# Thresholded attention with a SoLU feed-forward: q and k loaded in strips and turned on VectorE from the third batch on

## The chip, the cores and the metric

The kernel runs on one core of a Trainium2 chip. The time is the device time of one execution in microseconds (us). The kernel before was run three times: 895.34, 896.09 and 898.36 us, a median of 896.09 us.

## What is computed

For 8 batches of 8 heads, with q, k and v of 576 rows of 64 float32 each, attention keeps only the scores that lie within tau of their row's maximum. Its result is the input of a feed-forward block with a softmax-weighted activation and a layer norm:

```python
scores = scale * np.matmul(q, k.transpose(0, 1, 3, 2))          # scale = 1/8
thresh = np.max(scores, axis=-1, keepdims=True) - tau
scores = np.where(scores >= thresh, scores, -1000000000.0)
attn = np.exp(scores - np.max(scores, axis=-1, keepdims=True))
attn = attn / (np.sum(attn, axis=-1, keepdims=True) + 1e-09)
attn_out = np.matmul(attn, v)                                    # 8 x 8 x 576 x 64
x = attn_out.transpose(0, 2, 1, 3).reshape(4608, 512)
h = x @ w_in                                                     # 512 -> 1024
solu = h * softmax(h)
out = layer_norm(solu) * g_ln @ w_out                            # 1024 -> 512
```

## The kernel before

**Rounds.** The work is cut into 144 rounds (`slots`), 18 for each batch. Rounds 0 to 15 of a batch take one pair of heads and 128 of the first 512 query rows each (`kind` 0 and 1, `hp`, `r`); rounds 16 and 17 take the last 64 query rows of all heads (`kind` 2). In a round, `scores` (L412) makes the scores of both heads in two PSUM tiles `s_ps`, 128 x 576 each. `maxes` (L434, VectorE) finds each row's maximum and adds tau, `ramp` (L449, ScalarE) reads the scores a second time and pushes everything below the threshold far down, `exps` (L458, ScalarE) takes the exponential and its row sum. The score tiles are free for the next round once both ramps have read them. One round later `normalise` (L465 to L468, GpSimd) divides by the sum and `blocks` (L480, VectorE) turns the weights in blocks of 32 x 32 into T. After every second round T goes into its final place wT by four SyncE DMAs (L491). `attend_steps` (L516) multiplies wT by v some rounds later into `pv`, which ScalarE copies to `xh` or `xe` (L539).

**Feed-forward.** A tile of 128 tokens takes four rounds: two halves of h (`ff_h`, L572) and two halves of o (`ff_o`, L676). Between them lie the row maximum (L587), the exponential (L596, ScalarE), the product (L602), the statistics (L617, L618, then GpSimd), the norm (L638 on ScalarE, L643 on VectorE), a swap of halves by four SyncE DMAs (L654), and a 32 x 32 block transpose (L664). ScalarE copies the result out (L691) and SyncE stores it (L703). A pv product runs only in rounds without a half of o.

**q, k and v.** The matmuls need q and k with the 64 values of a row along the partitions. `load_one` (L129) brings four heads of q or k, rows of four tokens (1,024 bytes) to a partition, `load_ends` (L140) the last 64 rows in runs of 256 bytes, both on SyncE from the second batch on. They are turned on TensorE by 64 x 64 matmuls with the identity (`turn`, L282), 36 for each pair of heads (each shows as two records), into columns of the score tiles that the scores leave free. `q_item`, `k_item` and `e_item` then copy them out of PSUM: q times `scl` (the scale, with its sign, or 0) on ScalarE (L315) and VectorE (L319), k on both (L340), the ends on ScalarE (L356) and VectorE (L360). `load_v` brings v in one DMA of 128 rows and two of 64 rows with runs of 1,024 bytes (L159), and two with runs of 256 bytes (L164).

**What sets the order.** Every engine works through its own instructions in the order in which the main loop writes them. A round writes, in this order: `begin` jobs (the copy of the last o), scores with the items that `preps` has due, maxes, ramps, keeps (the copies of turned q and k), exps, `normalise` of the round before, `middle` jobs, the feed-forward quarter, the pv that is due, `blocks` of the round before, `late` jobs, and the loads that `load_at` lists for this round. `preps` lists for each pair of heads the round from which it may be turned, four to twelve rounds ahead of its first use. Buffers: `loads` holds two tiles each for q and k and three for v, `heads` seven each for the turned q and k.

The factor and the threshold are applied here:

```python
nc.vector.tensor_scalar(out=scl, in0=tau_t, scalar1=0.0, scalar2=SCALE, op0=ALU.is_ge, op1=ALU.mult)
...
nc.vector.tensor_tensor_reduce(out=w, in0=ps[:, 0:S], in1=(zero if loose else tau_t).to_broadcast([P, S]), scale=1.0, ...)
...
nc.scalar.activation(out=d["w"][x], in_=..., func=AF.Prelu, bias=d["nth"][x], scale=-1.0, alpha=1.0e30)
```

Of the kernel before, what the change touches and what calls it, by code (L numbers as in the profile page):

```python
# [8 lines left out]
F32 = mybir.dt.float32  # L9
# [11 lines left out]
def kernel(  # L21
# [56 lines left out]
    ntau = const.tile([P, 1], F32, name="ntau")  # L78
    scl = const.tile([P, 1], F32, name="scl")
    g_rows = const.tile([NC, P], F32, name="g_rows")  # L80
# [9 lines left out]

    halves = {}
    ends = {}
    pairs = {}
# [26 lines left out]
    def load_one(b, hf, nm, queue=None):  # L120
# [6 lines left out]
        for x, part in enumerate(parts):  # L127
# [5 lines left out]
            if hf == 0 and x == 0:  # L133
                if b not in ends:
                    ends[b] = loads.tile([P, H, D], F32, tag="ends", name="ends")
                load_ends(b, nm, slice(0, 2) if len(parts) > 1 else slice(0, H), queue)

    def load_ends(b, nm, of, queue):
        src, rows = {"q": (q, ROWS[0]), "k": (k, ROWS[1])}[nm]
        queue.dma_start(  # L140
            out=ends[b][rows, of], in_=src[b, of, SM:S, :].rearrange("h p d -> p h d")
        )
# [5 lines left out]
    def load_v(b, hf, parts=(0, 1, 2)):  # L148
        d = halves.setdefault((b, hf), {})
        hs = slice(4 * hf, 4 * hf + 4)  # L150

        if 0 in parts:
            d["v"] = loads.tile([P, 4, NK, D], F32, tag="v", bufs=3, name="v")
# [14 lines left out]
    def constants():  # L168

        nc.gpsimd.memset(lim, 0.0)  # L170
        nc.scalar.activation(out=ntau, in_=lim, func=AF.Exp)
        make_identity(nc, ident)
        nc.gpsimd.memset(mhalf, -0.5)
        nc.gpsimd.memset(mone, -1.0)
        nc.gpsimd.memset(zero, 0.0)
        nc.gpsimd.memset(lim, -896.0 * 8388608.0)

        nc.vector.tensor_scalar(  # L180
            out=scl, in0=tau_t, scalar1=0.0, scalar2=SCALE, op0=ALU.is_ge, op1=ALU.mult
        )
        nc.vector.tensor_scalar(
            out=tau_t, in0=tau_t, scalar1=0.0, scalar2=104.0, op0=ALU.max, op1=ALU.min
        )
        nc.vector.tensor_scalar(out=ntau, in0=tau_t, scalar1=-1.0, scalar2=None, op0=ALU.mult)

    def gains():
# [106 lines left out]
    def pair(i):  # L295
        if i not in pairs:
            pairs[i] = dict(
                qT=heads.tile([P, SM], F32, tag="qT", name="qT"),
                kT=heads.tile([P, S], F32, tag="kT", name="kT"),
                qe=heads.tile([P, ST], F32, tag="qe", name="qe"),  # L300
            )
        return pairs[i]

    def q_item(i, ts=slice(0, 4)):
# [8 lines left out]
        def keep(spare, x, r):  # L313
            if r == 0 or spare.get("eased"):
                nc.scalar.activation(  # L315
                    out=qT[:, r, ts], in_=seen(spare, r, x, n), func=AF.Copy, scale=scl
                )
            else:
                nc.vector.tensor_scalar(  # L319
                    out=qT[:, 1, ts], in0=seen(spare, 1, x, n), scalar1=scl, scalar2=None,  # L320
                    op0=ALU.mult,
                )

# [23 lines left out]
    def e_item(i):  # L347
# [6 lines left out]
        def keep(spare, x, r):  # L354
            if r == 0:
                nc.scalar.activation(  # L356
                    out=pair(i)["qe"], in_=seen(spare, 0, x, 1)[:, 0], func=AF.Copy, scale=scl
                )
            else:
# [63 lines left out]
    def maxes(s, loose):  # L423
# [4 lines left out]
        for ps in d["ps"]:  # L428
            if loose:
                nth = both[:, len(d["w"]) : len(d["w"]) + 1]  # L430
            else:
                nth = small.tile([P, 1], F32, tag="nth", name="nth")
            w = work.tile([P, S], F32, tag="w", bufs=4, name="w")
            nc.vector.tensor_tensor_reduce(  # L434
                out=w, in0=ps[:, 0:S], in1=(zero if loose else tau_t).to_broadcast([P, S]), scale=1.0, scalar=BIG,
                op0=ALU.add, op1=ALU.min, accum_out=nth,
# [10 lines left out]
    def ramp(s, x):  # L447
        d = live[s]
        nc.scalar.activation(  # L449
            out=d["w"][x], in_=d["w"][x] if d["loose"] else d["ps"][x][:, 0:S], func=AF.Prelu, bias=d["nth"][x], scale=-1.0,  # L450
            alpha=1.0e30,
# [43 lines left out]
    def attend_steps(key):  # L495
# [7 lines left out]
        for e in range(2) if kind == 2 else [None]:  # L503
            for m in range(NK):
                for u in range(2):
                    d, h0 = source(b * NP + (hp if e is None else e + 2 * u))
                    for h in range(2):
# [3 lines left out]
                        else:  # L511
# [4 lines left out]
                        nc.tensor.matmul(  # L516
                            out=to, lhsT=d["v"][ROWS[u], h0 + h, m ^ 4 * u if m < 8 else m],
                            rhs=rhs,
# [175 lines left out]
    def ff_store(t, last):  # L694
# [3 lines left out]
        else:  # L698
            b, kind, m = t
            rows = out[b * S : b * S + SM, :].rearrange("(p t) m -> t p m", t=4)  # L700
            rows = rows[2 * kind + m].rearrange("(r k) m -> k r m", r=2)
# [20 lines left out]
    preps = []  # L722
    for i in range(NP, NPAIR):
        b, hp = divmod(i, NP)
        if b == 1:
            at = (13, 15, 19, 20)[hp]
        else:
            at = PER * (b - 1) + ((6, 12, 16, 21) if b == 2 else (6, 9, 12, 17))[hp]
        preps += [
# [6 lines left out]
    load_at = {}  # L736
    for b in range(1, B):
        r = PER * (b - 1)

        for at, job, hf, what in (  # L740
            (-1 if b > 1 else 11, load_one, 0, "q"),
            (1 if b > 1 else 9, load_one, 0, "k"),
            (7 if b > 1 else 13, load_one, 1, "k"),
            (9 if b > 1 else 15, load_one, 1, "q"),
            (11 if b > 1 else 17, load_v, 0, (0,)),
            (13 if b > 1 else 19, load_v, 0, (1, 2)),
            (PER + 3, load_v, 1, (0,)),
            (PER + 5, load_v, 1, (1, 2)),
        ):
            load_at.setdefault(r + at, []).append(  # L750
                lambda b=b, job=job, hf=hf, what=what: job(b, hf, what)
            )

    with tc.manual_schedule():
# [29 lines left out]
        while True:  # L784
# [120 lines left out]
            if rnd - 1 in live:  # L905
                blocks(rnd - 1)
            for job in late.pop(rnd, []):
                job()
# [49 lines left out]
```

## Time and profile before

| | |
|---|---|
| median of three runs | 896.09 us (895.34 to 898.36) |
| the profiled execution | 897.51 us; its span, first to last instruction, 895.6 us |
| mean granted TensorE clock | 0.972 |
| DMA packets | 95,502, 154.61 MB, mean 173 GB/s |
| of these on SyncE's queue | 94,192, 150.09 MB |
| copies of turned q and k on ScalarE from PSUM (L315, L340, L356), mean | 475, 317 and 225, 339 ns |
| the same on VectorE (L319, L340, L360), mean | 479, 352 and 216, 215 ns |
| DMA of wT (L491), issue to landing | 3.9 / 5.7 / 9.9 us (least, median, most) |

A line of the profile names engine, source line, operation, the tile written and the tiles read. PE is TensorE, PEld its weight loads, DVE VectorE, ACT ScalarE, POOL GpSimd, SP SyncE; a "q" behind an engine is its sequencer, which waits, branches and issues DMAs. "idle before" is time in which the engine stood still ahead of the instruction, with what ended it. In the row of DMA each digit is the busy share of the DMA engines in one fortieth of the span, in tenths. Matmuls overlap each other, so the busy times of groups on PE can't be added to a time on the path.

### The profile page before, as it was taken

The page shows a single profiled execution, that of the slowest core. Times are in us where ns is not written, and L with a number is a line of the kernel's source. Part 1 is how long each engine was busy: PE and PEld are TensorE (multiplying, and loading weights), DVE is VectorE, ACT ScalarE, POOL GpSimd, SP SyncE. Part 2 cuts the span into 40 slices and gives each one's busy share as a digit, 9 for nine tenths or more (in the row PEclk, how much of TensorE's full clock was granted, in tenths as well). Part 3 has the DMA queues.
Part 4 walks back from the last instruction along what each step waited for, and adds up shares of the span by engine and source line. Part 5 has one row for each costly group of instructions (what it writes and reads, how often), then busy time and mean ns, then how long its engine had stood idle before and what let it go on. Part 6 is the DMA issues. An engine that isn't in the chain of part 4 may idle for free. (4 is left out here: it accounts for less than half of the span.)

```text
span 895.6 us, 39683 instructions
## 1 busy us (share of the span) xinstructions
PE 849.5 (95%) x17089; PEld 653.5 (73%) x17089; DVE 679.9 (76%) x1312; ACT 591.0 (66%) x1241; POOL 450.9 (50%) x871
## 2 busy tenths in 40 slices
PE   5668899999999999999999999999999999999997
PEld 3445577877677777777688887887778787777655
DVE  5999886888777778777777877777777877887351
ACT  5766776777767767776677776677766776676121
POOL 2546555555555555555645555555555555555120
PEclk9678899999999999999999999999999999999999
DMA  7999879786877777777777767866887766766322
GB/s 240 248 225 264 208 196 210 181 209 161 207 164 172 162 177 170 185 171 167 189 178 173 172 158 183 184 172 158 189 184 176 183 131 143 167 142 131 79 48 48
DMA packets 95502, 154.61 MB, mean 173 GB/s; under 512 B 27224, under 2 KB 69216, under 8 KB 95328
## 3 DMA queue, kind: packets, MB, share of 16 engines
q1 hardware_dynamic: 94192, 150.09, 71.8%
q8 instruction: 134, 2.20, 1.1%
q10 hardware_dynamic: 1136, 2.00, 0.7%
q14 instruction: 40, 0.33, 0.1%
HBM read 46.14 MB, written 9.44 MB: 62 GB/s over the span
## 5 line engine op out<-in xcount | busy, mean ns | idle before, releaser
L434 DVE CUSTOM_DVE_ANT_0 w<-s_ps,tau_t 128x576 f32<-128x576 f32 x280 | 200.7, 754 | 138.3 <-PE s_ps L412 114.4
L449 ACT ACTIVATE w<-s_ps,nth 128x576 f32<-128x576 f32 x280 | 202.0, 745 | 120.7 <-DVE nth L434 107.1
L676 PE MATMUL o_ps<-w,uT 64*64 64x256 f32 x4608 | 270.5, 376 | 2.1 <-issue 1.1
L676 PEld LDWEIGHTS o_ps<-w,uT 64*64 64x64 f32 x4608 | 229.8, 133 | 49.2 <-issue 10.8
L468 POOL TENSOR_SCALAR w<-w,sm 128x576 f32<-128x576 f32 x288 | 218.3, 770 | 14.3
L572 PE MATMUL h_ps<-w,xh 64*64 64x512 f32 x1856 | 222.2, 590 | 1.1 <-issue 1.1
L458 ACT ACTIVATE w<-w,ntau 128x576 f32<-128x576 f32 x288 | 220.4, 773 | 0.0
L480 DVE STREAM_TRANSPOSE T<-w 128x576 f32<-128x576 f32 x288 | 205.9, 751 | 5.9 <-POOL w L468 5.4
L516 PEld LDWEIGHTS pv<-wT,v 64*64 64x64 f32 x5760 | 173.1, 137 | 35.0 <-issue 17.5
L412 PE MATMUL s_ps<-kT,qT 64*64 64x512 f32 (+1 forms) x2048 | 176.4, 424 | 14.8 <-ACT w L449 13.8
L516 PE MATMUL pv<-wT,v 64*64 64x128 f32 (+1 forms) x5760 | 175.5, 266 | 6.3 <-issue 3.5
L572 PEld LDWEIGHTS h_ps<-w,xh 64*64 64x64 f32 x1856 | 119.9, 133 | 80.3 <-issue 47.8
L465 POOL TENSOR_SCALAR sm<-sm 128x2 f32<-128x2 f32 x144 | 35.9, 249 | 263.5 <-ACT w L458 260.6
L466 POOL TENSOR_TENSOR sm<-sm,mone 128x2 f32<-128x2 f32 x144 | 105.6, 733 | 12.0
L412 PEld LDWEIGHTS s_ps<-kT,qT 64*64 64x64 f32 x2048 | 70.0, 139 | 24.3 <-ACT w L449 20.0
L638 ACT ACTIVATE V<-u,nb,rs 128x1024 f32<-128x1024 f32 x36 | 44.7, 1241 | 52.6 <-POOL nb L628 52.6
L539 ACT COPY xh<-pv 128x256 f32<-128x256 f32 x64 | 23.7, 371 | 64.9 <-PE pv L516 64.9
L458 ACT ACTIVATION_READ_ACCUMULATOR w<-w,ntau 128x1 f32 x288 | 57.2, 199 | 0.0
L587 DVE TENSOR_REDUCE hm<-h_ps 128x1 f32<-128x1024 f32 x36 | 43.1, 1196 | 16.0 <-PE h_ps L572 10.7
L596 ACT ACTIVATE u<-h_ps,hm 128x1024 f32<-128x1024 f32 x36 | 40.3, 1119 | 19.5 <-DVE hm L587 11.7
L664 DVE STREAM_TRANSPOSE uT<-V 128x1024 f32<-128x1024 f32 x36 | 43.8, 1217 | 9.3 <-DMA V<-u 9.3
L602 DVE TENSOR_TENSOR u<-h_ps,u 128x1024 f32<-128x1024 f32 x36 | 42.8, 1190 | 10.1 <-ACT u L596 10.1
(81 smaller groups left out, 637.8 us busy)
## 6 DMA issues: line engine op xcount, KB each, us to landing
wT<-T SPq DMA_DIRECT2D x288, 288.0 KB, 5.7
V<-u SPq DMA_DIRECT2D x144, 64.0 KB, 3.6
out_dram<-ob SPq DMA_DIRECT2D x71, 128.0 KB, 2.8
v<-in_v_dram SPq DMA_DIRECT2D x16, 512.0 KB, 6.2
v<-in_v_dram SPq DMA_DIRECT2D x32, 256.0 KB, 5.8
q<-in_q_dram SPq DMA_DIRECT2D x15, 512.0 KB, 6.4
k<-in_k_dram SPq DMA_DIRECT2D x15, 512.0 KB, 6.8
raw<-in_moe_w_out_dram SPq DMA_DIRECT2D x8, 512.0 KB, 7.8
```

The lines of the kernel that those rows point to most:

```text
L412: nc.tensor.matmul(out=ps[h][ROWS[y], ks], lhsT=lhsT, rhs=d["kT"][ROWS[h], ks], start=True, stop=True,)
L434: nc.vector.tensor_tensor_reduce(out=w, in0=ps[:, 0:S], in1=(zero if loose else tau_t).to_broadcast([P, S]), scale=1.0, scalar=BIG, op0=AL ...
L449: nc.scalar.activation(out=d["w"][x], in_=d["w"][x] if d["loose"] else d["ps"][x][:, 0:S], func=AF.Prelu, bias=d["nth"][x], scale=-1.0, al ...
L458: nc.scalar.activation(out=w, in_=w, func=AF.Exp, bias=ntau, scale=1.0, accum_out=sm[:, x : x + 1])
L466: nc.gpsimd.tensor_tensor(out=sm, in0=sm, in1=mone, op=ALU.pow)
L468: nc.gpsimd.tensor_scalar(out=w, in0=w, scalar1=sm[:, x : x + 1], scalar2=1.0, op0=ALU.mult, op1=ALU.mult)
L480: nc.vector.transpose(out=T[:, :, r, h, :], in_=w)
L516: nc.tensor.matmul(out=to, lhsT=d["v"][ROWS[u], h0 + h, m ^ 4 * u if m < 8 else m], rhs=rhs, start=m == 0, stop=m == NK - 1,)
L572: mm = nc.tensor.matmul(out=h[ROWS[y], f], lhsT=x[ROWS[r], c, ROWS[y]], rhs=w1_parts[ROWS[r], c, part ^ r], start=part == 0 and c == 0, st ...
L638: nc.scalar.activation(out=V, in_=u, func=AF.Identity, bias=nb, scale=rs)
L664: nc.vector.transpose(out=uT, in_=d["V"].rearrange("p y (m x) -> p m y x", x=32))
L676: nc.tensor.matmul(out=d["o"][ROWS[z], 512 * r : 512 * r + 256], lhsT=d["uT"][ROWS[r], m].rearrange("p y x -> p (y x)"), rhs=w2[ROWS[r], m ...
```

## The change

From the third batch on (`b > 1`), q and k no longer come in whole rows. `load_blocks` loads one pair of heads at a time: four DMAs for q on SyncE and four for k on ScalarE's queue. Each fills 32 partitions with 18 strips of 32 values (128 bytes), 576 descriptors of 128 bytes. `turn_blocks` turns a tile of 128 x 576 by one VectorE block transpose, straight into the tile that the scores read; the last 64 query rows are now the end of the same tile. The loads stand at rounds 1, 5, 9 and 13 after the start of the batch before (batches counted from 0; two rounds later for even ones), at the end of the round; the turn of q three rounds later, k four. v comes in two DMAs with runs of 2,304 bytes, at rounds 17 and 21 (again two later for even batches), and the order of the rows of v and of the stored result follows.

q is no longer multiplied by the scale: the copies that remain in batches 0 and 1 are plain, `maxes` takes tau divided by the scale (`tau_s`) and multiplies by SCALE, `ramp` multiplies by -SCALE. Where tau is negative, `tau_t` becomes at least 2^120.

The diff, without the parts that only follow (tile declarations, the first two batches' unchanged tables):

```diff
@@ -135,6 +136,25 @@
                     ends[b] = loads.tile([P, H, D], F32, tag="ends", name="ends")
                 load_ends(b, nm, slice(0, 2) if len(parts) > 1 else slice(0, H), queue)
 
+    def load_blocks(i, nm, queue):
+        b, hp = divmod(i, NP)
+        src, names = {"q": (q, "(j p) a -> p j a"), "k": (k, "(p j) a -> p j a")}[nm]
+        d = strips.setdefault(i, {})
+        d[nm] = loads.tile([P, 4, 4, D], F32, tag=nm, name=nm)
+        flat = d[nm].rearrange("p h t d -> p (h t d)")[:, 0:S]
+        for g in range(4):
+            y, x = divmod(g, 2)
+            queue.dma_start(
+                out=flat[32 * g : 32 * g + 32].rearrange("p (j a) -> p j a", a=32),
+                in_=src[b, 2 * hp + y, :, 32 * x : 32 * x + 32].rearrange(names, **(
+                    dict(p=32) if nm == "q" else dict(j=NB)
+                )),
+            )
+
+    def turn_blocks(i, nm):
+        flat = strips[i].pop(nm).rearrange("p h t d -> p (h t d)")[:, 0:S]
+        nc.vector.transpose(out=pair(i)["q" if nm == "q" else "kT"], in_=flat)
+
     def load_ends(b, nm, of, queue):
         src, rows = {"q": (q, ROWS[0]), "k": (k, ROWS[1])}[nm]
         queue.dma_start(
@@ -149,6 +169,15 @@
         d = halves.setdefault((b, hf), {})
         hs = slice(4 * hf, 4 * hf + 4)
 
+        if b > 1:
+            if 0 in parts:
+                d["v"] = loads.tile([P, 4, NK, D], F32, tag="v", bufs=3, name="v")
+            for part in parts:
+                nc.sync.dma_start(
+                    out=d["v"][ROWS[part]].rearrange("p h m d -> p h (m d)"),
+                    in_=v[b, hs].rearrange("h (p m) d -> p h (m d)", m=NK),
+                )
+            return
         if 0 in parts:
             d["v"] = loads.tile([P, 4, NK, D], F32, tag="v", bufs=3, name="v")
         rest = v[b, hs, 0:SM, :].rearrange("h (p t) d -> p h (t d)", t=4)
@@ -178,12 +207,18 @@
 
 
         nc.vector.tensor_scalar(
-            out=scl, in0=tau_t, scalar1=0.0, scalar2=SCALE, op0=ALU.is_ge, op1=ALU.mult
+            out=ntau, in0=tau_t, scalar1=0.0, scalar2=2.0**120, op0=ALU.is_lt, op1=ALU.mult
         )
         nc.vector.tensor_scalar(
             out=tau_t, in0=tau_t, scalar1=0.0, scalar2=104.0, op0=ALU.max, op1=ALU.min
         )
+        nc.vector.tensor_scalar(
+            out=tau_t, in0=tau_t, scalar1=ntau, scalar2=None, op0=ALU.max
+        )
         nc.vector.tensor_scalar(out=ntau, in0=tau_t, scalar1=-1.0, scalar2=None, op0=ALU.mult)
+        nc.vector.tensor_scalar(
+            out=tau_s, in0=tau_t, scalar1=1.0 / SCALE, scalar2=None, op0=ALU.mult
+        )
 
     def gains():
         tag, g_ps = take("g_ps")
@@ -294,10 +329,10 @@
 
     def pair(i):
         if i not in pairs:
+            both = heads.tile([P, S], F32, tag="qT", name="qT")
             pairs[i] = dict(
-                qT=heads.tile([P, SM], F32, tag="qT", name="qT"),
+                q=both, qT=both[:, 0:SM], qe=both[:, SM:S],
                 kT=heads.tile([P, S], F32, tag="kT", name="kT"),
-                qe=heads.tile([P, ST], F32, tag="qe", name="qe"),
             )
         return pairs[i]
 
@@ -312,14 +347,9 @@
 
         def keep(spare, x, r):
             if r == 0 or spare.get("eased"):
-                nc.scalar.activation(
-                    out=qT[:, r, ts], in_=seen(spare, r, x, n), func=AF.Copy, scale=scl
-                )
+                nc.scalar.copy(out=qT[:, r, ts], in_=seen(spare, r, x, n))
             else:
-                nc.vector.tensor_scalar(
-                    out=qT[:, 1, ts], in0=seen(spare, 1, x, n), scalar1=scl, scalar2=None,
-                    op0=ALU.mult,
-                )
+                nc.vector.tensor_copy(out=qT[:, 1, ts], in_=seen(spare, 1, x, n))
 
         return n, make, keep
 
@@ -432,7 +460,7 @@
                 nth = small.tile([P, 1], F32, tag="nth", name="nth")
             w = work.tile([P, S], F32, tag="w", bufs=4, name="w")
             nc.vector.tensor_tensor_reduce(
-                out=w, in0=ps[:, 0:S], in1=(zero if loose else tau_t).to_broadcast([P, S]), scale=1.0, scalar=BIG,
+                out=w, in0=ps[:, 0:S], in1=(zero if loose else tau_s).to_broadcast([P, S]), scale=SCALE, scalar=BIG,
                 op0=ALU.add, op1=ALU.min, accum_out=nth,
             )
             d["nth"].append(nth)
@@ -447,7 +475,7 @@
     def ramp(s, x):
         d = live[s]
         nc.scalar.activation(
-            out=d["w"][x], in_=d["w"][x] if d["loose"] else d["ps"][x][:, 0:S], func=AF.Prelu, bias=d["nth"][x], scale=-1.0,
+            out=d["w"][x], in_=d["w"][x] if d["loose"] else d["ps"][x][:, 0:S], func=AF.Prelu, bias=d["nth"][x], scale=-1.0 if d["loose"] else -SCALE,
             alpha=1.0e30,
         )
 
@@ -514,7 +542,7 @@
                             )
                             rhs = wT[ROWS[u], :, m, e, h]
                         nc.tensor.matmul(
-                            out=to, lhsT=d["v"][ROWS[u], h0 + h, m ^ 4 * u if m < 8 else m],
+                            out=to, lhsT=d["v"][ROWS[u], h0 + h, m ^ 4 * u if m < 8 and b < 2 else m],
                             rhs=rhs,
                             start=m == 0, stop=m == NK - 1,
                         )
@@ -697,7 +725,9 @@
             rows = out.rearrange("(b s) m -> s b m", s=S)[SM:S, 2 * t[0] : 2 * t[0] + 2]
         else:
             b, kind, m = t
-            rows = out[b * S : b * S + SM, :].rearrange("(p t) m -> t p m", t=4)
+            rows = out[b * S : b * S + SM, :].rearrange(
+                "(p t) m -> t p m" if b < 2 else "(t p) m -> t p m", t=4
+            )
             rows = rows[2 * kind + m].rearrange("(r k) m -> k r m", r=2)
         for z in range(2):
             (nc.scalar if last and z else nc.sync).dma_start(
@@ -720,12 +750,8 @@
 
 
     preps = []
-    for i in range(NP, NPAIR):
-        b, hp = divmod(i, NP)
-        if b == 1:
-            at = (13, 15, 19, 20)[hp]
-        else:
-            at = PER * (b - 1) + ((6, 12, 16, 21) if b == 2 else (6, 9, 12, 17))[hp]
+    for i in range(NP, 2 * NP):
+        at = (13, 15, 19, 20)[i - NP]
         preps += [
             (at, 3, lambda i=i: k_item(i, slice(0, 3)), i),
             (at, 1, lambda i=i: k_item(i, slice(3, 4)), i),
@@ -734,21 +760,38 @@
         ]
 
     load_at = {}
-    for b in range(1, B):
+    turn_at = {}
+    for at, job, hf, what in (
+        (11, load_one, 0, "q"),
+        (9, load_one, 0, "k"),
+        (13, load_one, 1, "k"),
+        (15, load_one, 1, "q"),
+        (17, load_v, 0, (0,)),
+        (19, load_v, 0, (1, 2)),
+        (PER + 3, load_v, 1, (0,)),
+        (PER + 5, load_v, 1, (1, 2)),
+    ):
+        load_at.setdefault(at, []).append(
+            lambda job=job, hf=hf, what=what: job(1, hf, what)
+        )
+    for b in range(2, B):
         r = PER * (b - 1)
-
-        for at, job, hf, what in (
-            (-1 if b > 1 else 11, load_one, 0, "q"),
-            (1 if b > 1 else 9, load_one, 0, "k"),
-            (7 if b > 1 else 13, load_one, 1, "k"),
-            (9 if b > 1 else 15, load_one, 1, "q"),
-            (11 if b > 1 else 17, load_v, 0, (0,)),
-            (13 if b > 1 else 19, load_v, 0, (1, 2)),
-            (PER + 3, load_v, 1, (0,)),
-            (PER + 5, load_v, 1, (1, 2)),
-        ):
-            load_at.setdefault(r + at, []).append(
-                lambda b=b, job=job, hf=hf, what=what: job(b, hf, what)
+        even = 2 * (b % 2 == 0)
+        for hp in range(NP):
+            at = r + 1 + even + 4 * hp
+            load_at.setdefault(at, []).append(
+                lambda i=b * NP + hp: (
+                    load_blocks(i, "q", nc.sync), load_blocks(i, "k", nc.scalar)
+                )
+            )
+            at = max(at + 3, r + 17 if hp == NP - 1 else 0)
+            for x, nm in enumerate("qk"):
+                turn_at.setdefault(at + x, []).append(
+                    lambda i=b * NP + hp, nm=nm: turn_blocks(i, nm)
+                )
+        for hf in range(2):
+            load_at.setdefault(r + 17 + even + 4 * hf, []).append(
+                lambda b=b, hf=hf: load_v(b, hf, (0, 1))
             )
 
     with tc.manual_schedule():
@@ -904,7 +947,7 @@
                     ready.append((rnd + 1, [(b, kind, 0), (b, kind, 1)]))
             if rnd - 1 in live:
                 blocks(rnd - 1)
-            for job in late.pop(rnd, []):
+            for job in late.pop(rnd, []) + turn_at.pop(rnd, []):
                 job()
             if rnd == 3:
                 gains()
```

More of the change, by code (lines that the diff above doesn't have):

```diff
@@ L78 @@
     ntau = const.tile([P, 1], F32, name="ntau")
-    scl = const.tile([P, 1], F32, name="scl")
+    tau_s = const.tile([P, 1], F32, name="tau_s")
     g_rows = const.tile([NC, P], F32, name="g_rows")
@@ L91 @@
     halves = {}
+    strips = {}
     ends = {}
@@ L355, in keep @@
             if r == 0:
-                nc.scalar.activation(
-                    out=pair(i)["qe"], in_=seen(spare, 0, x, 1)[:, 0], func=AF.Copy, scale=scl
-                )
+                nc.scalar.copy(out=pair(i)["qe"], in_=seen(spare, 0, x, 1)[:, 0])
             else:
```

## The prediction

> **What bounds the kernel now.** I read the page first, then the waits, then the busy times by window, then the timelines of ScalarE and SyncE.
>
> The page's head, and two rows of the groups with shapes kept apart (busy us, mean ns, then idle time before):
>
> ```profile
> span 895.6 us, 39683 instructions
> PE   849.5 (95%) x17089; PEld 653.5 (73%) x17089; DVE 679.9 (76%) x1312; ACT 591.0 (66%) x1241; POOL 450.9 (50%) x871
> ...
> DMA  7999879786877777777777767866887766766322
> ```
> ```profile
> L282 PE MATMUL s_ps<-ident,k 64*64 64x64 f32 x896 | 25.5, 222 | 3.6 <-ACT w L449 3.3 <-DVE both L434 0.2
> L282 PE MATMUL s_ps<-ident,q 64*64 64x64 f32 x896 | 23.4, 222 | 6.2 <-ACT qe L356 4.8 <-ACT w L449 1.0 <-DVE both L434 0.3
> L480 DVE STREAM_TRANSPOSE T<-w 128x576 f32<-128x576 f32 x288 | 205.9, 751 | 5.9 <-POOL w L468 5.4
> ```
>
> TensorE is never idle outside the first and last slices: it sets the time. A round (one slot of 144) is scores, then a quarter of a feed-forward tile, then perhaps pv. I call rounds by their number modulo 4: 3 and 0 hold the halves of h (L572) with a pv, 1 and 2 the halves of o (L676). The windows run over four rounds each, from round kind 2 to the next (columns: length, busy time and count per engine, clock, DMA share, GB/s):
>
> ```profile
> 566.70:589.88 23.18, 23.18 (x509) 19.22 (x505) 17.91 (x36) 16.41 (x35) 12.13 (x25) 1.00 0.84 210
> 589.88:612.64 22.76, 22.76 (x477) 18.32 (x473) 17.84 (x35) 16.10 (x34) 12.12 (x25) 1.00 0.70 157
> 658.43:681.18 22.75, 22.75 (x478) 18.31 (x474) 17.77 (x35) 16.10 (x34) 12.12 (x25) 1.00 0.81 190
> 772.01:793.61 21.60, 21.60 (x405) 17.04 (x401) 17.25 (x31) 15.30 (x30) 12.49 (x25) 1.00 0.77 173
> 793.61:815.22 21.61, 21.61 (x406) 17.05 (x401) 17.25 (x32) 15.24 (x30) 12.50 (x25) 1.00 0.62 135
> ```
>
> The last two lie in batch 7, where no q or k is left to turn: 72 matmul records fewer, and TensorE still full. So the trace holds its own test of what the transposes are worth. What stands near the bound is seen in ScalarE's timeline at a round of kind 1 and the next, and in SyncE's beside it:
>
> ```profile
> 586.41 1.42 ACT L449 ACTIVATE w<-s_ps,nth 128x576 f32<-128x576 f32 x2 [0.19 <-DVE nth L434]
> 587.73 0.77 ACT L458 ACTIVATE w<-w,ntau 128x576 f32<-128x576 f32 x1
> ...
> 590.75 1.42 ACT L449 ACTIVATE w<-s_ps,nth 128x576 f32<-128x576 f32 x2 [1.40 <-DVE nth L434]
> ```
> ```profile
> 582.53 3.34 SPq L491 DMA_DIRECT2D wT<-T  x4
> 585.92 0.71 SPq L159 DMA_DIRECT2D v<-in_v_dram  x1
> 594.13 3.52 SPq L491 DMA_DIRECT2D wT<-T  x4
> ```
>
> ScalarE has 1.40 us to spare before round 2's ramps; those end at 592.2, and TensorE is through its o quarter at about 593.2 and must then have the score banks. So the ramps of a kind 2 round may start some 1.0 us late, and every us beyond stops TensorE.
>
> **What the Trainium skill says.** (1) "Perfetto Trace Analysis", section "Per-engine timelines": a ScalarE instruction is pushed into a wait queue and the sequencer goes on, but a DMA's semaphore wait is served by the sequencer itself before the reported start. So a DMA on ScalarE's queue that waits holds back everything after it, yet can itself be issued while earlier activations run. The trace agrees for SyncE (195.8 us of its waiting stands before L491); it shows no waiting DMA on ScalarE in the middle of the kernel. (2) "DMA: Bandwidth & Descriptors", section "Issuing engines are not separate DMA queues": k on ScalarE's queue uses the same 16 DMA engines. (3) Same page, "Why small descriptors are slow": size/32+3 cycles, 11 for 256 bytes, so 7 for 128 by its formula. In this trace the 256-byte packets took 18 ns at the median. (4) "VectorE: DVE Perf Modes", "The three transpose paths": VectorE turns 32x32 blocks only; the row of L480 prices one of 128x576 at 751 ns, or 0.715 us back to back.
>
> **The change part by part, in us, 24 pairs (batches 2 to 7).**
>
> *TensorE.* 24 x 72 records of L282 go. By busy time they are 30 ns each (60.8 us / 2016), 52 us in all, but they overlap their neighbours. Window against window, a pair costs 1.15 to 1.58; seventeen such windows in a row from batch 3 on (less 0.5 to 1.4 for those with an end-of-batch pv) come to 17 us over 21.6 each, 1.0 to 1.1 per pair. I take 26 (bounds 24 and 31).
>
> *Evacuations.* ScalarE loses 0.475 + 0.317 + 0.225 + 0.339 = 1.36 per pair (L315, L340, L356), VectorE 0.479 + 0.352 + 0.216 + 0.215 = 1.26. Nothing on the path: batch 7 runs without them and its period is TensorE's.
>
> *VectorE's turns.* Two of 0.75 per pair, net +0.24 per pair against the lost copies, but in other rounds: q in kind 0, k in kind 1. Kind 0 then holds 1.45 (L434) + 1.43 (L480) + 1.2 (L664) + 1.19 (L587) + 0.75 = 6.0 of 6.5. Kind 1 holds 1.45 + 1.43 + 1.18 (L602) + 0.75 = 4.8 in 4.3: round 2's maxima start 0.5 late, its ramps too, inside the 1.0. Queued behind are the statistics and L480 of round 2, so wT of round 2 is issued 0.5 later for a pv that comes 0.6 sooner; its slack in batch 7 is 0.1 to 1.6. I put 0 to 0.8 per period here.
>
> *DMA bytes.* 24 x 8 x 576 = 110,592 descriptors of 128 bytes come, 12,288 of 1 KB and 6,144 of 256 bytes go. Per period 288 per engine; at 20 ns 6 us, at 39 (a 256-byte burst in company) 11. The DMA share of 0.62 to 0.84 counts packets that wait for each other, so it fits at 20. I take no cost of its own, and put the upper end in a rival. v becomes two DMAs of 576 KB in place of five; SyncE issues 20 loads per batch for 16, +24 x 0.9 us, beside its idle time.
>
> *k on ScalarE's queue.* Four issues after the exponentials of round kind 1, at 0.45 to 0.72 as at the kernel's start, 0.65 taken. In themselves hidden behind the two exponentials. But the built program gives DMAs eight semaphores in turn, and each DMA waits for the landing of the one eight before it. I followed those waits:
> - In 13 of the 24 places the fourth k DMA waits at most for wT of round 0, usually its fourth DMA. In the window shown that one landed at 590.42: k goes out until 591.1, the ramps start at 591.2 and TensorE loses nothing. In other rounds it lands up to 3 us later. Mean 0.5 with VectorE's lateness, 13 x 0.5 = 6.5 (0 to 16).
> - In rounds 41, 73, 77, 109 and 113 it waits for the second v DMA, issued just before on SyncE behind wT. Today a v group of 1,152 KB in such a round is complete 7.6 to 9.0 after the first L434 of the round; beside k strips I take 9.2. Then 0.65 for the issue and 1.42 for the ramps: 11.3, where TensorE is ready at 7.65. Loss 3.6 x 5 = 18 (7 to 25).
> - In rounds 57 and 93 it waits for the first v DMA, 7.2: 9.3, loss 1.7 x 2 = 3.5.
> - Rounds 21, 25, 29, 33 come before the regular order, two wait for q strips of the same round: 4 in all (0 to 8).
>
> Behind the waiting k stand the next ramps, and for those TensorE's next scores, which come first in its order. A loss in an o round is not made good, since TensorE is full in the others.
>
> *No scale on q, tau_s.* The score maximum and the ramp take the factor as an operand they already have: 0. Two more VectorE operations of 0.154 at the start lie beside the first loads.
>
> **Sum.** -26 + 6.5 + 18 + 3.5 + 4 = +6 on the profiled execution of 897.5 us (span 895.6 and 1.9 around it): 903.5. The median of the runs, 896.1, is 1.4 lower: forecast 902.
>
> **Rivals.**
> - *A, faster: v and wT land before ScalarE needs its queue.* The place is the fourth k DMA of rounds 41, 73, 77, 109, 113; below 6.1 us after the round's first L434 its wait costs nothing. For it: one 512 KB v in the window shown landed at 591.52, 5.97 after; wT is issued 0.6 sooner without the copies. Then -26 + 6 = -20: 876. It decides for faster when the mean of these five losses is under about 1.5 and the 13 others cost under 0.5; half way lies 888.
> - *B, much slower: the DMA engines become the bound.* At 39 ns a descriptor, 11 us per period on top of a share of 0.62 x 21.6 = 13.4 plus v overfills 21.6, wT lands late and pv waits: 1 us more per pair than the forecast, 902 + 24 = 926. Against it: packets of 256 bytes at 18 ns.
> - *C, gain and loss cancel* within 0.3%, about what a measurement can tell from no change: 896.
> - That the transposes stay is excluded: the built order has no L282 of batches 2 to 7.
>
> **Chances.** Forecast (slower, 899 to 912) 0.38; A 0.34; C 0.14; B 0.14. Faster by over 0.3% 0.34, within 0.14, slower 0.52. The range leaves a tenth on each side: 874 (A nearly whole) to 924 (B's middle). The forecast's own range is 899 to 912.
>
> **What would show it.** Right: no matmul of L282 after batch 2's first pairs; a wait of TensorE's scores for ScalarE's ramp (today 13.8 and 20.0 us in the waits) grown by 15 to 35 us; in the timeline k DMAs on ScalarE whose start stands at the landing of wT or v; periods of 21.6 to 22.3 without v and near 25 with it. Wrong on A: ramps of kind 2 start under 6.1 us after the round's first L434 everywhere. Wrong on B's side: pv waiting for wT (2.3 us today) by 20 us or more, DMA share above 0.9.

## The result and the profile after

The changed kernel takes 950.48 us at the median of six runs (945.49 to 957.06), beside 897.64 us (895.34 to 900.35) for the kernel before on the same chips: a ratio of 1.059, 95% interval 1.0540 to 1.0641. It is slower by 5.9%. The forecast was 902 us with a range up to 924: the sign was right, the size was not.

The page's head, two DMA queues (packets, MB, share of 16 engines), and three rows of the groups with shapes kept apart:

```profile
span 951.9 us, 36177 instructions
...
PE   851.3 (89%) x15361; PEld 628.6 (66%) x15361; DVE 688.7 (72%) x1266; ACT 564.7 (59%) x1145; POOL 457.8 (48%) x871
...
PEclk9688998979989999999899999999899999999998
DMA  7999968767998889888978889988968888666322
...
q10 hardware_dynamic: 57968, 9.08, 7.6%
```
```profile
L508 DVE STREAM_TRANSPOSE T<-w 128x576 f32<-128x576 f32 x288 | 207.1, 754 | 13.8 <-POOL w L496 12.9 <-issue 0.4
...
L156 DVE STREAM_TRANSPOSE qT<-q 128x576 f32<-128x576 f32 x24 | 18.1, 755 | 0.0
...
L156 DVE STREAM_TRANSPOSE kT<-k 128x576 f32<-128x576 f32 x24 | 18.0, 751 | 0.0
```

1,728 matmul records fewer run on TensorE, the 48 turns cost the 0.75 us they were priced at, and yet TensorE is busy 851 us as before, in a span 56 us longer. So it stands still, and part of its work has become slower. The 57,968 packets of ScalarE's queue (q10), nearly all k strips, took on the mean 0.076 x 16 x 951.9 / 57,968 = 20 ns.

The waits (us in total, times, longest):

```profile
PEld s_ps L440 <- ACT w L477: 68.8, 48, 9.4
...
PE s_ps L440 <- ACT w L477: 54.0, 41, 8.5
...
ACT w L477 <- DMA k<-in_k_dram: 34.8, 6, 8.8
...
ACT w L477 <- DMA v<-in_v_dram: 24.4, 3, 8.3
...
PE pv L544 <- DMA wT<-T: 10.6, 7, 5.5
```

TensorE's scores wait for ScalarE's ramp (L477; in the kernel before 20.0 us on PEld and 13.8 on PE), and the ramp waits for DMAs that it does not read: they only stand ahead of it in ScalarE's order. Rounds 73, 74 and 75, with v, above rounds 81, 82 and 83 without (length, busy time and count of each engine, clock, DMA share, GB/s):

```profile
454.16:458.67 4.51, 4.51 (x88) 4.14 (x84) 4.51 (x9) 3.44 (x8) 1.35 (x4) 1.00 0.92 215
458.67:469.36 10.69, 5.94 (x82) 4.46 (x78) 4.12 (x10) 3.55 (x7) 3.98 (x10) 0.80 1.14 164
469.36:478.66 9.30, 8.45 (x199) 5.28 (x195) 3.88 (x7) 4.10 (x9) 3.95 (x8) 0.86 0.69 171
...
514.37:518.88 4.51, 4.51 (x88) 4.13 (x84) 4.51 (x9) 3.44 (x8) 1.36 (x4) 1.00 0.92 204
518.88:523.35 4.47, 4.47 (x82) 3.91 (x78) 4.11 (x10) 2.65 (x5) 3.14 (x7) 1.00 1.16 111
523.35:529.70 6.35, 6.35 (x124) 4.51 (x120) 4.11 (x8) 5.10 (x11) 4.34 (x10) 1.00 0.79 158
```

ScalarE's timeline of round 73 and SyncE's beside it show why:

```profile
456.48 0.57 ACTq L147 DMA_DIRECT2D k<-in_k_dram  x1
...
457.79 7.92 ACTq L147 DMA_DIRECT2D k<-in_k_dram  x3
465.81 1.37 ACT L477 ACTIVATE w<-s_ps,nth 128x576 f32<-128x576 f32 x2 [7.85 <-DMA v<-in_v_dram]
```
```profile
450.55 3.58 SPq L519 DMA_DIRECT2D wT<-T  x4
454.17 2.75 SPq L176 DMA_DIRECT2D v<-in_v_dram  x2
456.96 6.48 SPq L147 DMA_DIRECT2D q<-in_q_dram  x4
466.88 3.56 SPq L519 DMA_DIRECT2D wT<-T  x4
```

The second of these lines holds three issues of 0.57 us each and the waits between them. The fourth k DMA leaves 10.98 us after the round's first L462, when the second v DMA has landed; rounds 77, 109 and 113 read 10.96, 11.37 and 11.43. The ramps of round 74 follow it at 465.81, and TensorE, done at 462.0, stands still until 466.60. Then a part that the forecast did not have: the second window below runs at half the clock.

```profile
458.67:465.10 6.43, 3.33 (x62) 2.88 (x54) 4.12 (x10) 0.00 (x0) 3.47 (x8) 1.00 1.16 203
465.10:471.90 6.80, 5.15 (x32) 2.87 (x36) 2.54 (x6) 6.09 (x11) 2.40 (x4) 0.50 1.03 149
471.90:478.66 6.76, 5.91 (x187) 4.00 (x183) 1.34 (x3) 1.56 (x5) 2.05 (x5) 1.00 0.62 152
```

The Trainium skill describes this in "TensorE: Matmul & The Clock Gate", section "HAM oscillation": its rule is to leave TensorE no idle gap above some 3.4 us, or the clock is throttled again. This trace agrees: between 100 us and the last 20 us the kernel before has no halved stretch, the changed one has seven, each behind a standstill of 4.1 to 8.5 us, and each 3.4, 6.8 or 10.2 us long. Over all runs the clock was halved behind shorter standstills too: 18 of 22 between 2.4 and 3.4 us. There the measurement decides (last section).

Round by round against the kernel before, the 56.3 us of longer span are: +28.0 up to the end of round 41 (mainly rounds 22, 26, 30, 39 and 40), +37.0 in rounds 57 to 59, 74, 75, 78, 79, 94, 110, 111, 114 and 115, -11.8 in all others up to 129, +3.2 behind the last round.

### The profile page after: what moved, and what is told of

The parts are those of the page before. It is cut to its first block, busy times and chain, and to the rows that moved or that the text cites. A ratio compares the mean times of both kernels' runs of the same rounds, so it can differ in the third digit from the quotient of the medians.

```text
span 951.9 us, 36177 instructions
## 1 busy us (share of the span) xinstructions
PE 851.3 (89%) x15361; PEld 628.6 (66%) x15361; DVE 688.7 (72%) x1266; ACT 564.7 (59%) x1145; POOL 457.8 (48%) x871
## 3 DMA queue, kind: packets, MB, share of 16 engines
q10 hardware_dynamic: 57968, 9.08, 7.6%
## 5 line engine op out<-in xcount | busy, mean ns | idle before, releaser
L462 DVE CUSTOM_DVE_ANT_0 w<-s_ps,tau_s 128x576 f32<-128x576 f32 x280 | 199.6, 749 | 157.5 <-PE s_ps L440 139.8
L477 ACT ACTIVATE w<-s_ps,nth 128x576 f32<-128x576 f32 x280 | 196.5, 741 | 184.7 <-DVE nth L462 93.9
L704 PE MATMUL o_ps<-w,uT 64*64 64x256 f32 x4608 | 273.3, 380 | 4.6 <-DVE uT L692 2.5
L704 PEld LDWEIGHTS o_ps<-w,uT 64*64 64x64 f32 x4608 | 238.7, 134 | 47.5 <-issue 18.2
L440 PE MATMUL s_ps<-kT,qT 64*64 64x512 f32 (+1 forms) x2304 | 207.8, 438 | 57.0 <-ACT w L477 54.0
L496 POOL TENSOR_SCALAR w<-w,sm 128x576 f32<-128x576 f32 x288 | 225.4, 794 | 14.3
L600 PE MATMUL h_ps<-w,xh 64*64 64x512 f32 x1856 | 227.5, 606 | 2.8 <-ACT ob L719 1.7
L508 DVE STREAM_TRANSPOSE T<-w 128x576 f32<-128x576 f32 x288 | 207.1, 754 | 13.8 <-POOL w L496 12.9
L544 PEld LDWEIGHTS pv<-wT,v 64*64 64x64 f32 x5760 | 169.4, 137 | 49.8 <-issue 36.9
L600 PEld LDWEIGHTS h_ps<-w,xh 64*64 64x64 f32 x1856 | 115.4, 138 | 96.4 <-issue 85.8
L440 PEld LDWEIGHTS s_ps<-kT,qT 64*64 64x64 f32 x2304 | 81.1, 143 | 76.2 <-ACT w L477 68.8
```

What stands on the lines that cost most here:

```text
L440: nc.tensor.matmul(out=ps[h][ROWS[y], ks], lhsT=lhsT, rhs=d["kT"][ROWS[h], ks], start=True, stop=True,)
L477: nc.scalar.activation(out=d["w"][x], in_=d["w"][x] if d["loose"] else d["ps"][x][:, 0:S], func=AF.Prelu, bias=d["nth"][x], scale=-1.0 if ...
L496: nc.gpsimd.tensor_scalar(out=w, in0=w, scalar1=sm[:, x : x + 1], scalar2=1.0, op0=ALU.mult, op1=ALU.mult)
L508: nc.vector.transpose(out=T[:, :, r, h, :], in_=w)
L544: nc.tensor.matmul(out=to, lhsT=d["v"][ROWS[u], h0 + h, m ^ 4 * u if m < 8 and b < 2 else m], rhs=rhs, start=m == 0, stop=m == NK - 1,)
L600: mm = nc.tensor.matmul(out=h[ROWS[y], f], lhsT=x[ROWS[r], c, ROWS[y]], rhs=w1_parts[ROWS[r], c, part ^ r], start=part == 0 and c == 0, st ...
```

## The experiments

Theory 1: k DMAs on ScalarE's queue, each of which waits for the landing of the DMA eight before it on the two queues together, hold up the ramps. Rival 2: the short descriptors themselves hold up the DMA engines. Ratios are to the kernel before, run beside each.

**e1, k on SyncE's queue**

```diff
-                    load_blocks(i, "q", nc.sync), load_blocks(i, "k", nc.scalar)
+                    load_blocks(i, "q", nc.sync), load_blocks(i, "k", nc.sync)
```

> The changed kernel with the k strips issued by SyncE instead of ScalarE, all else the same. Theory 1 (the k DMAs wait on ScalarE's queue for v and wT to land, the ramps behind them come late, TensorE stands still): the stalls of TensorE's scores on the ramp in rounds 22, 30, 58, 74, 78, 94, 110 and 114 go, about 40 of the 53 us lost; SyncE now waits in ScalarE's place and wT behind it comes later, which gives back 5 to 15: 900 to 920 us. Rival 2 (the 110,592 short descriptors themselves hold up the DMA engines): the same descriptors move, 945 to 955 us, with TensorE waiting as long as before, for wT.

Measured 919.97 us, ratio 1.0261 (1.0214 to 1.0309). The stalls on the ramp go, and a wait for wT comes in their place:

```profile
PE pv L544 <- DMA wT<-T: 26.9, 18, 5.4
...
PEld s_ps L440 <- ACT w L477: 22.0, 20, 4.0
```

That is the upper end of theory 1's range. The same descriptors move, so rival 2 falls as the account of these 30 us. In round 73 the k DMAs now leave SyncE 10.9 to 14.0 us after the round's first L462, and the next wT behind them after 14.7 us, where it was 12.7.

**e2, v in other rounds**

```diff
-            load_at.setdefault(r + 17 + even + 4 * hf, []).append(
+            load_at.setdefault((r + 11 + even) if hf == 0 else (r + 23 - even), []).append(
```

> The changed kernel with the v DMAs moved out of the rounds that load strips (to rounds of kind 3, two before or two after), k still on ScalarE's queue. The fourth k DMA then stands eight DMAs behind wT of the round before, as in the 13 undisturbed places. Theory 1: the losses of rounds 58, 74/75, 78/79, 94, 110/111 and 114 (together 37 us) go, the early ones of rounds 22 to 40 stay: 908 to 918 us. Rival 2 (short descriptors slow all DMA): same bytes in the same descriptors, 942 to 955 us.

Measured 967.02 us, 1.0765 (1.0713 to 1.0818): a miss, on the other side. The losses of the v rounds did not go but moved, to rounds 50, 62, 70, 86, 98, 106, 114 and 122 with 3.3 to 5.7 us each. v now stands ahead of wT of kind 0; that wT lands after 9.4 to 10.7 us where 5 to 7 are usual, and the k DMAs of the next round wait for it. ScalarE at round 49:

```profile
320.25 4.71 ACTq L147 DMA_DIRECT2D k<-in_k_dram  x4
325.06 1.37 ACT L477 ACTIVATE w<-s_ps,nth 128x576 f32<-128x576 f32 x2 [6.62 <-DMA wT<-T]
```

The mechanism stands; which landing is waited for had changed.

**e3, no strip loads**

```diff
-                lambda i=b * NP + hp: (
+                lambda i=b * NP + hp: i == 2 * NP and (
...
-        flat = strips[i].pop(nm).rearrange(...)
+        flat = strips[2 * NP][nm].rearrange(...)
```

> The changed kernel without the loads of q and k from the second pair of batch 2 on: only the first pair's strips are loaded, and the VectorE turns of all later pairs read these, so 23 of 24 pairs' q and k are left out. It keeps the turns, v in its new form and the missing TensorE work. Theory 1 and the forecast's term of 26 us for TensorE: all losses but that of round 22 go, 873 to 884 us. Rival 3 (the gain on TensorE was never there, or the turns on VectorE eat it): 893 to 905 us.

Measured 888.78 us, 0.9899 (0.9863 to 0.9935). The gain on TensorE is there, but smaller than expected: rounds 42 to 129 are 15.5 us shorter than before for 20 pairs, with one standstill of 2.4 us in round 75 among them, for which the profile names no cause (last section). Round 22 keeps its loss (+7.5).

**e4, the standstills filled**

```diff
+                if rnd in (74, 78, 110, 114):
+                    tag, f_ps = take("fill")
+                    for x in range(28):
+                        ...
+                        nc.tensor.matmul(out=f_ps[...], lhsT=ident[ROWS[h], 0:64], rhs=w1[ROWS[h], 0, 0:512], ...)
+                    pairs_free.append(tag)
                 scores(rnd, items)
```

> The changed kernel with 28 matmuls of 64x512 (about 4.1 us) into a free PSUM tile that nothing reads, ahead of the scores of rounds 74, 78, 110 and 114, where TensorE stood still for 4.6 to 5.1 us. It only adds work. Theory of the clock (standing still for over 4 us halves TensorE's clock for the next 6.8 us, some 3.4 us lost each time): no halved clock after these four, 936 to 944 us. Rival (the halved clock costs nothing, as the later rounds wait for something else): 949 to 956 us.

Measured 944.4 us, 1.0514 (1.0479 to 1.0549), 0.4 us above the range expected for the clock. The changed kernel's interval begins at 1.0540, so the two touch, and the rounds must decide. Rounds 73, 74 and 75 in three windows:

```profile
453.30:464.50 11.20, 10.18 (x134) 5.25 (x129) 4.58 (x10) 3.58 (x8) 3.23 (x6) 1.00 1.05 204
464.50:468.98 4.48, 4.48 (x84) 2.85 (x80) 4.13 (x9) 2.88 (x6) 1.26 (x4) 1.00 0.79 78
468.98:475.38 6.40, 6.40 (x196) 4.02 (x192) 4.05 (x7) 4.76 (x9) 3.83 (x9) 1.00 0.79 161
```

The extra work took 6.2 us and ran while k waited for v: rounds 73 and 74 together last 15.7 us as against 15.2. Round 75 then takes 6.4 instead of 9.3 at full clock, rounds 79 and 111 6.3 and 6.4 instead of 7.6 and 10.4; the four halved stretches are gone. The rounds behind the four standstills are 8.7 us shorter in all, although only useless matmuls came in. About 3 us of that are two standstills without a named cause (0.85 us in round 75, 2.2 in round 111) that this run does not have. So the halved clock is a cost of its own, an estimated 5 to 6 us in these four places.

**e5, k two rounds later**

```diff
-                    load_blocks(i, "q", nc.sync), load_blocks(i, "k", nc.scalar)
...
+            load_at.setdefault(at, []).append(lambda i=b * NP + hp: load_blocks(i, "q", nc.sync))
+            load_at.setdefault(at + 2, []).append(lambda i=b * NP + hp: load_blocks(i, "k", nc.scalar))
```

> The changed kernel with each pair's four k DMAs issued two rounds later, at the end of rounds of kind 3, still on ScalarE's queue; q, v and the turns stay where they are. They then stand eight DMAs behind wT of a kind 2 round and the V swap, not behind v, and the ramps behind them belong to a kind 0 round, where TensorE needs the score banks some 3 us later. Theory 1 (what costs time is which landing a k DMA on ScalarE's queue waits for, and how soon TensorE needs the ramps behind it): 892 to 912 us. Rival 2 (the short descriptors themselves): no difference, 942 to 955 us.

Measured 944.43 us, 1.0485 (1.0434 to 1.0536), inside rival 2's numbers, but not by its cause: e1 and e8 move the same descriptors. In kind 3 the k DMAs stand behind the copy of pv, mostly start about 1 us after the next round's maxima and issue until 4 to 7 us after them; ScalarE's ramps wait for them 15 times, 86.0 us in all. The round of kind 1 behind grows by 1.1 us in nearly every period, that of kind 0 often by 1 to 4. I had allowed kind 0 some 3 us; four issues of 0.6 us with their waits, ahead of its ramps, are more.

**e6, only v in the new form, no scale.** Loads and turns of q and k are again those of the kernel before:

```diff
-    for i in range(NP, 2 * NP):
+    for i in range(NP, NPAIR):
...
```

> Only v in two DMAs of 2,304-byte runs, at the new rounds, and the missing scale on q; q and k of all batches come in rows and are turned on TensorE as before. Theory 1: v and the scale cost nothing by themselves, 893 to 901 us. Rival 4 (two 576 KB DMAs of 64 rows each, issued late and landing after 9 to 11 us, hold up the pv products or wT on their own): 903 to 925 us.

Rows of k and of v no longer pair up in this kernel; only its time is read. Measured 922.5 us, 1.0209 (1.0126 to 1.0291), with four executions from 911 to 927 us, of which the longest was traced. So v's new form costs something, as rival 4 says, but not cleanly: some of the new v rounds are old rounds of q or k, whose 512 KB are issued right behind v (rounds 53, 73, 89, 109). And the cause is not rival 4's. In the places of loss (rounds 39, 56, 76, 92, 112) the profile shows no wait of TensorE for v or wT; it stops in the middle of a pv product or of an h half, with no releaser. Round 56:

```profile
337.67 2.10 PE L544 MATMUL pv<-wT,v 64*64 64x64 f32 x128 [0.17 <-issue]
343.05 0.58 PE L544 MATMUL pv<-wT,v 64*64 64x64 f32 x10 [3.28 <-issue]
```

The last section says where these standstills stand.

**e7, from the fourth batch on.** The third batch is loaded, turned and stored as in the kernel before:

```diff
-    for b in range(2, B):
+    for b in range(3, B):
...
```

> The changed kernel with strips, turns and the new v only from the fourth batch on; the third batch comes and is turned as before. Takes away the four k loads of rounds 21 to 33, whose waits stood at about +28 us by round 41, and four pairs' gain on TensorE (some 4). Theory 1: 920 to 932 us, rounds 42 to 129 as in the changed kernel. If the early loss has another cause than these loads: 944 to 955 us.

Measured 923.16 us, 1.0260 (1.0188 to 1.0331). Up to round 41 it is 1.4 us ahead of the kernel before, where the changed kernel is 28.0 behind; rounds 42 to 129 lose 23.9, beside 25.1. So the early loss comes from the third batch's loads.

**e8, k on GpSimd's queue**

```diff
-                    load_blocks(i, "q", nc.sync), load_blocks(i, "k", nc.scalar)
+                    load_blocks(i, "q", nc.sync), load_blocks(i, "k", nc.gpsimd)
```

> The changed kernel with the k strips on GpSimd's queue. The built program gives its DMAs semaphores of their own, so that no k DMA waits for a landing of v, wT or q. Theory 1: no stall of TensorE on a ramp behind a k DMA. If an issue on GpSimd takes about 1 us[...], 880 to 905 us; if GpSimd has to write the 576 descriptors of each DMA itself and takes several us for it, its multiplications by the row sums come late, then wT, and pv waits: 905 to 940 us. Rival 2 (short descriptors hold up the DMA engines): 942 us or more.

Measured 911.97 us, 1.0129 (1.0064 to 1.0194). An issue takes GpSimd 0.70 us, for which 880 to 905 us were expected: a miss by 7. The ramp's stalls are back at the level of before (14.4 and 20.9 us). 10.5 us are lost up to round 41 and 1.9 from there to round 129: pv waits for wT in rounds 40, 60, 80 and 116, TensorE stands without a named cause in rounds 39, 75 and 111, and these eat what it gains.

**e9 and e10, v earlier as well; e10 from the fourth batch on**

```diff
-            load_at.setdefault(r + 17 + even + 4 * hf, []).append(
-                lambda b=b, hf=hf: load_v(b, hf, (0, 1))
+        for at, hf, part in ((11, 0, 0), (13, 0, 1), (PER + 3, 1, 0), (PER + 5, 1, 1)):
+            load_at.setdefault(r + at, []).append(lambda b=b, hf=hf, part=part: load_v(b, hf, (part,)))
```

> k strips on GpSimd's queue, and v, still in 2,304-byte runs, at the rounds of the kernel before: one 576 KB DMA each at rounds 11, 13, 21 and 23 after the start of the batch before, no longer two together two or three rounds ahead of the first use. What was lost with k on GpSimd stood in the v rounds and the two after (39/40, 60, 75/76, 80, 96, 111, 116: some 35 us, TensorE's pv waiting for v or wT). Theory 5 (v lands late, and delays wT that is issued behind it): half of it and more returns, 885 to 902 us. Rival (wT is late because SyncE waits for q strips): 905 to 916 us.

> The same, with strips, turns and the new v only from the fourth batch on. The early loss (11 us by round 41 with k on GpSimd) goes, four pairs' gain on TensorE (some 4) too. Theory 5: 875 to 893 us, faster than both kernels. Rival: 893 to 905 us.

Measured 901.45 us, 1.0020 (0.9999 to 1.0040), and 898.58 us, 0.9999 (0.9980 to 1.0018). e9 is at the end of theory 5's range: v's rounds were worth some 10 us, and the waits of pv for wT fall from 15.3 us in e8 to 6.0. e10 missed it; it ties with the kernel before.

**e11 and e12, v directly behind wT; e12 with k two rounds later.** Against e10; the lines that move k in e12 are as in e5, on GpSimd's queue:

```diff
-        for at, hf, part in ((11, 0, 0), (13, 0, 1), (PER + 3, 1, 0), (PER + 5, 1, 1)):
+        for at, hf, part in ((10, 0, 0), (12, 0, 1), (PER + 4, 1, 0), (PER + 6, 1, 1)):
```

> The kernel of the run before it (k strips on GpSimd, from the fourth batch on), with the four v DMAs at rounds 10, 12, 22 and 24 after the start of the batch before: each then stands directly behind wT in SyncE's order, and two rounds ahead of the next wT, not directly ahead of one. Theory 5 (wT lands late where a fresh v DMA is ahead of it, then pv waits in rounds of kind 0): the waits of rounds 52, 80, 116, 124 and 104 (12 us) go, 882 to 892 us. Rival (the strips of q and k alone fill the DMA engines in these rounds): 894 to 902 us.

> The same, and the k strips two rounds later, at the end of rounds of kind 3, so that only the q strips stand in the round ahead of wT of kind 2. If the strips' own traffic makes wT late: 3 to 8 us under the run without it, 878 to 889 us. If not: within 3 us of it, or more where GpSimd's four issues hold up the kind 0 round.

Measured 917.45 us, 1.0199 (1.0159 to 1.0239), and 959.37 us, 1.0685 (1.0651 to 1.0720): both wrong. v now precedes the V swap instead of wT, and VectorE's turn of V, then TensorE's o, wait for that. In e11:

```profile
DVE uT L692 <- DMA V<-u: 71.1, 28, 5.5
...
PE o_ps L704 <- DVE uT L692: 14.8, 9, 2.4
```

In e10 the two are 44.9 and 1.7 us.

**e13, only v on GpSimd's queue**

```diff
-                nc.sync.dma_start(
+                nc.gpsimd.dma_start(
                     out=d["v"][ROWS[part]].rearrange("p h m d -> p h (m d)"),
```

> The changed kernel with only the two v DMAs of each half batch moved to GpSimd's queue, at the same rounds; k stays on ScalarE. v's DMAs have semaphores of their own there, so no k DMA is eight behind a v DMA; the bytes, the descriptors and the times of the loads are the same. Theory 1: the losses of rounds 58, 74/75, 78/79, 94, 110/111 and 114 (37 us) go, the early ones of rounds 22 to 30 stay, and with the first pv of a batch waiting for v (2 to 4 us a batch, five batches) it gives 915 to 930 us. Rival 2 or 5 (v's traffic as such, not the wait for it): 940 us or more.

Measured 927.83 us, 1.0323 (1.0276 to 1.0371). Same bytes, same rounds; two issues move from SyncE to GpSimd, and nothing is eight behind v any more. Rounds 42 to 129 lose 3.4 us instead of 25.1, and up to 41 still 23.0. Round 73 on ScalarE:

```profile
449.89 3.66 ACTq L147 DMA_DIRECT2D k<-in_k_dram  x2
453.65 1.37 ACT L477 ACTIVATE w<-s_ps,nth 128x576 f32<-128x576 f32 x2 [4.92 <-DVE T L508]
```

The ramps start 8.7 us after the round's first L462 (444.97) instead of 11.65. v itself lands no sooner: its second DMA 12.0 to 13.0 us after the first L462 of rounds 73, 77 and 109, while the fourth k DMA leaves after 5.8 to 6.3 us. So the wait for v, not v's traffic, made most of the v rounds' loss.

**e14, k and v on GpSimd's queue, otherwise as e10.** Edit: the line of e13, on e10, which has k there already.

> The run with k on GpSimd, v at its earlier rounds and strips from the fourth batch on (898.6 us), now with v on GpSimd's queue as well. On SyncE's queue nothing waits for a landing of v any more; the traffic is the same. If the turn of eight semaphores holds the rest of the loss: 882 to 891 us, faster than both kernels. If sharing the DMA engines does: 894 to 905 us.

Measured 908.51 us, 1.0114 (1.0078 to 1.0149), worse than e10: the turn of eight does not hold the rest of the loss. Sharing the DMA engines is left as a likely cause, since wT and the V swap land late with no wait for v ahead of them, but no run isolates it, and this time lies outside the 894 to 905 us given for it too. No version that loads all of q and k beats the kernel before.

## Why the prediction was wrong, step by step

| Term | Forecast | Measured |
|---|---|---|
| TensorE without the transposes, 24 pairs | -26 | e3: -15.5 for 20 pairs, 0.78 each (0.95 without the standstill in round 75): 19 to 23 for 24 |
| 13 places that wait for wT only | +6.5 | -11.8 against e3's -15.5: +3.7 |
| rounds 41, 73, 77, 109, 113 | +18 | +31.9 in four of them (2.2 of it without a named cause), nothing in 41 |
| rounds 57 and 93 | +3.5 | +5.1 |
| rounds 21, 25, 29, 33 | +4 | +28.0 up to round 41, with what follows from it |
| end | 0 | +3.2, cause open |
| sum | +6 | +56.3 |

**Right.** What bounds the kernel before, the price of 20 ns a descriptor on the mean (rival B's 39 was not seen), that VectorE's turns hide (e3 keeps them and gains), and the mechanism: a k DMA on ScalarE's queue waits for the DMA eight before it, and the ramps behind it stop TensorE. The places named for v are the places of loss, but for round 41. That the waits for wT alone cost little also held.

**The v rounds: the right mechanism, wrongly sized.** Two terms were too small. In rounds 73, 77, 109 and 113 the second v DMA landed after 11.0 to 11.4 us, not 9.2: "beside k strips I take 9.2" put little on top of the 7.6 to 9.0 of the old v. And behind the standstill the clock halves: round 75 took 9.3 us against 6.35 for its like. "Loss 3.6 x 5" became 9.1, 6.3, 10.5 and 6.0; e4 shows the clock's part, e13 the wait's. No case of the forecast reckoned with the clock. Rival A would have needed v by 6.1. Round 41 shows that it was right so far: v went out 4.2 us ahead of that round's first L462, the fourth k DMA left 6.4 us after it, when v had landed, and nothing was lost.

**The early rounds: the step that failed most.** "4 in all (0 to 8)" was set without following each wait, because these rounds "come before the regular order". The four k DMAs of round 21 start 0.1 to 7.4 us after round 22's first L462. The second and third leave when the second and fourth wT DMA of that round have landed, the last when a q strip of its own round has; wT and that strip had been issued behind batch 1's v. The fourth of round 29 starts 13.6 us after that round's first L462. Round 22 grew by 6.4, round 30 by 7.9, and rounds 39 and 40 lost 9.4 more, to ScalarE's late copy of o (L719) and to a late wT. e7 returns all of it.

**The gain on TensorE** was 1.1 a pair from the windows of the kernel before; 0.8 to 0.95 came. The range ended at 924 because its cases varied one cost at a time; losses of one root (late landings ahead of ramps, with the clock behind them) grew together. Two slips of arithmetic change nothing: half way between 876 and 902 is 889, not 888, and rival B's sum is 926, where the range took 924 as its middle.

## What to carry to other kernels

A DMA put on a computing engine's queue is priced by the latest landing that it may have to wait for, and by what stands behind it on that engine: list for each such DMA the one whose semaphore it takes over, and do so for the irregular rounds first. Where TensorE stands still for more than some 2.4 us, add the half clock to the loss (28 of 34 cases from 2.4 to 4.0 us in these runs, all 30 above). Moving a large load by one or two rounds did not remove the wait here but gave it to whatever is issued next (wT, then the V swap).

## What the runs showed of the hardware that was not expected

- **Halved clock.** Over the 16 profiles, from 110 us on and without the last 30, TensorE's standstills of 0.8 us and more had a halving during them or within 3.5 us behind them in 0 of 54 cases up to 1.1 us, 10 of 75 from 1.1 to 2.4, 28 of 34 from 2.4 to 4.0, and 30 of 30 above.
- **Standstills at every 256th instruction.** Of the same 193 standstills, the profile names no releaser ("issue") for 56. 54 of these stand at one place: where the count of TensorE's matmuls and weight loads from the start, divided by 256, leaves 193. Of the 137 with a releaser 3 do. Each of the 54 ends 1.25 to 1.83 us after the end of a packet of 16 KB in the queue that the page calls "instruction":

```profile
q8 instruction: 121, 1.98, 0.9%
```

121 packets for 30,936 matmuls and weight loads are one for 256. So TensorE most likely waited for its own next instructions, which come as DMA packets too; no run tests it, nor why they came late. It makes 0.8 us in the kernel before, 5.2 in the changed one, 7.3 in e10 (of 14.1 us of such standstills), and all 21.3 in e6.
- **Strips on GpSimd's queue** show in e8 as 4,608 packets (q0, 4.6% of the engines): 1,536 each of 4,096, 512 and 4 bytes, one of each for a DMA and engine, so that 36 strips of 128 bytes went in two packets. ScalarE's queue has 55,296 packets of 128 bytes among its 57,968 (q10, 7.6%). The strips landed no sooner: 5.8 us at the median beside 5.4.
